# A residual block's second-norm sums and output scalings moved to ScalarE, with new plan latencies and weight slots

## The chip, the cores and the metric

The kernel runs on one core of a Trainium2 chip. The metric is device time in microseconds; lower is better. The core has five engines, each with its own in-order queue: TensorE (PE, matmuls; its weight loads are shown as PEld), VectorE (DVE), ScalarE (ACT), GpSimd (POOL) and SyncE (SP, which here issues most DMAs).

## The reference

A residual block of a diffusion network on two images of 512 channels, 64 x 64 pixels, in bf16:

```python
    B, C, H, W = x.shape                      # 2, 512, 64, 64
    G, eps = 4, 1e-5
    def gn(z, gamma, beta):                   # group norm, 4 groups of 128 channels
        ...
    def conv3(z, w):                          # 3x3 convolution, padding 1
        ...
    h = conv3(_silu(gn(x, g1, be1)), w1)
    emb = _silu(t_emb) @ w_emb
    h = h + emb.reshape(B, C, 1, 1)
    h = conv3(_silu(gn(h, g2, be2)), w2)
    return x + h
```

Each of the four groups is one block of 128 channels, so a group's mean and variance are sums over the free dimension of one tile followed by a sum over its 128 partitions.

## The kernel before, in words

**Arithmetic.** Both convolutions use a Winograd scheme along the rows: four output rows from six input rows, with the three taps along x kept as they are. A chunk is 32 rows of one image, so there are four chunks per layer (`chunks`, idx 0 to 3, two for each image). Layer 0 is the first convolution, layer 1 the second. For each chunk and each of the four blocks of output channels (`ot`) there is a set (`one_set`): six row positions, each a sum over four input blocks and three taps, 12 matmuls of 128 x 512. Positions come in pairs, (1,3), (2,4) and (0,5); a pair fills one of three accumulator tiles `acc` in PSUM, used in turn (`row_pair`, `next_acc`). In a plain set this makes 72 matmuls. In a column set (all of layer 1, and chunk 2 of layer 0, `COL0`), positions 0 and 5 are made by a second Winograd scheme along x, with half as wide matmuls (`col_pair`): 80 matmuls in all. In the last chunk of layer 1 the pair (1,3) is made that way too (`more_pair`): 88.

**The transformed input.** For each chunk and input block, `v_block` makes a block of `Vbuf`: group norm and Silu in one ACT instruction into `a_tmp` (`silu_rows`), then eight or more additions on DVE through `vt`, with some scalings on ACT or DVE (`make_v`). `Vbuf` holds two chunks.

**The transformed weights.** `u_blocks` takes two weight blocks at a time from `stage` (two buffers), transposes them on PE (nine transposes of 128 x 128 into `xa` and `xb`, line 348), copies them out with ACT (line 447), with scaled copies by 0.25 and 0.5 also read from PSUM by ACT (line 449), and forms the positions by additions on DVE into `Upair`, 22 slots of 128 columns per block. The middle tap and its half live in a temporary, `g1t`. `u_cols` and `u_more` form the slots for the column schemes. Layer 1's weights go where layer 0's were, as the last chunk of layer 0 is done with them.

**A set's output.** ACT evacuates pair (1,3) to `m1` and pair (2,4) to `w_`, scaled by 1/6. DVE forms sum and difference in `w_`; they are t1, t2 (sums) and s1, s2 (differences). Output rows 1 and 2 of each tile are s1 + 2 s2 and t1 + 4 t2; rows 0 and 3 are t1 + t2 and s1 + 8 s2 plus positions 0 and 5. In layer 0 these additions are `scalar_tensor_tensor` instructions on DVE that also give the sum of what they write (`acc_sum`, a column of `ssum`; line 292, each followed by an accumulator read), four in a plain set and six in a column set; those for positions 0 and 5 read `acc` in PSUM. In layer 1, where no sums are wanted, the factors 2, 4 and 8 are separate scalings on DVE (`ts`, line 284). After a layer-0 set the tile `y` goes out to `h_scr` by DMA, and ACT squares it in place for the sum of squares (`ssq`). In layer 1, POOL adds x by an accumulating DMA, and SP sends the result out.

**Statistics.** `first_stats` handles the first image's input with matmuls on PE (line 840). `second_stats` handles the second image's: for each input block and each half of 2048 pixels, one ACT Identity with a sum and one ACT Square with a sum, read from `V` into a scratch tile. `stats2` turns `ssum` and `ssq` into layer 1's norm. `norm` sums over partitions by a small fp32 matmul (line 364), followed by small DVE operations and a power on POOL (lines 377, 381) that end in the scale `sc` and the bias `nb`.

**The order.** Nothing is ordered by hand. Every instruction is first entered in a `_Plan` with its engine, an estimated cost, a latency `lat`, and what it reads and writes. `issue` runs a list scheduling eight times, keeps the order with the shortest planned span, and emits it: each engine's queue is thus fixed before the run. `lead` raises a node's priority. `wait` is added to the time at which a node may start after one of another engine. The parameters' DMAs on the ACT queue are planned with a latency of 2.0. The last set of all is `final_set`, written apart: it takes positions 2 and 4 one at a time, in that order, so that little is left behind the last matmul.

Of the kernel before, what the change touches and what calls it, by code (L numbers as in the profile page):

```python
# [18 lines left out]
class _Node:  # L19
    __slots__ = ("eng", "cost", "lat", "emit", "due", "idx", "pred", "succ", "left", "fin", "nbytes", "lead", "wait")  # L20


class _Plan:
# [39 lines left out]
    def add(self, eng, cost, emit, reads=(), writes=(), group=None, lat=0.09, due=None, nbytes=0, lead=0.0,  # L63
            wait=0.05):
        n = _Node()
        n.eng, n.cost, n.lat, n.emit, n.due, n.idx = eng, cost, lat, emit, due, len(self.nodes)
        n.nbytes, n.lead, n.wait = nbytes, lead, wait
# [24 lines left out]
        return n  # L92

    def _run(self, nodes, pred, succ, prio, look):
# [8 lines left out]
        while len(order) < len(nodes):  # L103
# [15 lines left out]
            if n.nbytes:  # L119
                dma = max(dma, s + 1.6) + n.nbytes / self.RATE  # L120
                fin = dma + 0.6
# [38 lines left out]
def kernel(  # L160
# [34 lines left out]
    NSL = 22  # L195
    COL0 = (2,)
# [55 lines left out]
    def small(shape, name):  # L252
        count["small"] += 1
        return sb(shape, f"{name}{count['small']}", F32)
# [41 lines left out]
    def act(out, in_, func=None, scale=1.0, bias=None, accum=None, **kw):  # L296
# [14 lines left out]
        plan.add("ACT", c, emit, reads, [out] + ([] if accum is None else [accum]), **kw)  # L311
# [44 lines left out]
    def norm(layer, b, c0, n, me, ps=None):  # L356
# [8 lines left out]
        plan.add("PE", 0.3, mm, [me[:], ones_neg[:]], tok if ps is None else [ps], lat=0.2, lead=100.0)  # L365
# [26 lines left out]
    Ut = [[[None] * CT for _ in range(CT)] for _ in range(2)]  # L392

# [6 lines left out]
    def u_cols(layer, ot, c0, n, tmp):  # L400
        U = u_pair(layer, ot, c0)
        two = lambda first: slots(U, c0, n, first, [[1, 2 * P]])
        ck = view(tmp, 0, [[2 * NKX * P, n], [1, 2 * P]])
        tt(ck, two(0), two(4), ALU.add)
        tt(two(6), ck, two(2), ALU.subtract)
        tt(two(20), ck, two(2), ALU.add)

    def u_more(layer, ot, c0, n):
        U = u_pair(layer, ot, c0)
        g = lambda kx: slots(U, c0, n, 8 + 4 * kx, [[2 * P, 2], [1, P]])  # L410
        ck = view(g1t, 0, [[2 * P, n], [P, 2], [1, P]])
        tt(ck, g(0), g(2), ALU.add)
        tt(slots(U, c0, n, 2, [[P, 2], [1, P]]), ck, g(1), ALU.subtract)
        tt(g(1), g(1), ck, ALU.add)

    def u_load(layer, ot, ct, **kw):
        k = count["blk"]
        count["blk"] += 1
        wn = stage[k % 2]
# [3 lines left out]
    def u_blocks(layer, ot, c0, loads, tmp=None, dve=False, act_scale=True):  # L423
# [3 lines left out]
        taps = [[P, NKX], [1, P]]  # L427
        for i, wn in enumerate(loads):
            ct = c0 + i
            Ut[layer][ot][ct] = U[:, ct % 2]  # L430
            one = lambda first, step: slots(U, ct, 1, first, [[step * P, NKX], [1, P]])
            raw = slots(U, ct, 1, 0, [[1, 6 * P]])
            mid = [view(tmp, (2 * i + h) * NKX * P, [[1, NKX * P]]) for h in range(2)]
            wv = wn[:].rearrange("p (c ky kx) -> p kx ky c", ky=3, kx=3)
            pa, pb = XBank("xa", [NKX, 2, P], BF16), XBank("xb", [NKX, P], BF16)
            transposes(pa, [((lambda t, kx=kx, j=j: t[:, kx, j, :]), wv[:, kx, 2 * j, :])
                            for kx in range(NKX) for j in range(2)], ["xa"], [wn[:]], 0.45)
            transposes(pb, [((lambda t, kx=kx: t[:, kx, :]), wv[:, kx, 1, :]) for kx in range(NKX)],
                       ["xb"], [wn[:]], 0.23)

            def copy(out, bank, tok, size_, sel=lambda t: t[:], scale=None):
# [3 lines left out]
                elif scale is None:  # L445
                    plan.add("ACT", 0.07 + size_ * 0.0008,
                             lambda: nc.scalar.copy(out=out, in_=sel(bank.get())), [tok], [out])  # L447
                else:
                    plan.add("ACT", 0.07 + size_ * 0.0008, lambda: nc.scalar.activation(
                        out=out, in_=sel(bank.get()), func=ACT.Copy, scale=scale), [tok], [out])  # L450
# [7 lines left out]
        g = lambda j: slots(U, c0, n, j, [[2 * P, NKX], [1, P]])  # L458
        up = lambda j: slots(U, c0, n, 8 + j, [[4 * P, NKX], [1, P]])
        m = lambda h: view(tmp, h * NKX * P, [[2 * NKX * P, n], [P, NKX], [1, P]])  # L460
        if dve or not act_scale:
            ts(up(3), g(0), 0.25)
            ts(m(1), m(0), 0.5)
        tt(up(1), g(0), g(1), ALU.add)
        tt(up(0), up(1), m(0), ALU.add)
        tt(up(1), up(1), m(0), ALU.subtract)
        tt(up(3), up(3), g(1), ALU.add)
        tt(up(2), up(3), m(1), ALU.add)
        tt(up(3), up(3), m(1), ALU.subtract)
# [3 lines left out]
    def u_tap(U, pos, kx):  # L473
        if pos in (0, NPOS - 1):
            return U[:, 2 * kx + (1 if pos else 0), :]
        return U[:, 8 + 4 * kx + pos - 1, :]

    def u_col(U, j, c):
        return U[:, (0, 20, 6, 4)[c] + j, :]

    def u_col_more(U, j, c):
        return U[:, (8 + 2 * j, 12 + 2 * j, 2 + j, 16 + 2 * j)[c], :]
# [82 lines left out]
    ssum = [small([CT, sum(6 if is_col(0, b, c) else 4 for c in range(NCH))], "ssum") for b in range(B)]  # L565
# [72 lines left out]
    def final_set(U, V):  # L638
# [15 lines left out]
        for k, pos in enumerate((2, 4)):  # L654
# [4 lines left out]
            if k == 0:  # L659
                for i in range(2):  # L660
                    tt(sd[:, i], sd[:, i], view(w_, i, [[2 * NFREE, 2], [2, NC]]), ALU.add)
# [12 lines left out]
        for h in range(2):  # L674
            o = view(y, h * n, [[(TH - 1) * W, 2], [TH * W, TR // 2], [1, W]])
            tt(o, o, view(w_, NFREE + h * NFREE // 2, [[2 * NFREE, 2], [1, NFREE // 2]]).rearrange(
# [4 lines left out]
    def one_set(layer, idx, ot, U, V):  # L681
# [7 lines left out]
        base = sum(6 if is_col(0, b, c) else 4 for c in range(ch))  # L689
# [4 lines left out]
        else:  # L694
            a = row_pair((1, 3), U, V, col, gid, 1)
            act(m1[:], a[:], scale=KAPPA)
# [23 lines left out]
        w03 = t4(w_[:, :, 0])  # L720
        if col and layer == 0:
            for k in range(2):
                tt(sd[:, k], sd[:, k], view(w_, k, [[2 * NFREE, 2], [2, NC]]), ALU.add)
        if not col:
            a = row_pair((0, 5), U, V, col, gid, 1)
            for i, f in enumerate((0, TH - 1)):
                stt(y4[:, f], t4(a[:, i:i + 1])[:, 0], 1.0, w03[:, i], ALU.mult, ALU.add, accum=acc_sum(2 + i))
        else:
            aa = col_pair((0, 3), U, V, gid)
            if layer == 0:  # L730
                for j in range(2):
                    for k, op in ((0, 1.0), (1, -1.0)):
# [3 lines left out]
                            accum=acc_sum(2 + 2 * j + k))  # L736
# [9 lines left out]
        y03 = y4[:, 0:TH:TH - 1]  # L746
        tt(y03, y03, w03, ALU.add)
# [3 lines left out]
    def emb_all():  # L751
# [5 lines left out]
        for e0 in range(0, ET, per):  # L757
            n = min(per, ET - e0)
            wt = stage[count["blk"] % 2]
            count["blk"] += 1  # L760
# [42 lines left out]
    for i, prm in enumerate((g1, be1, g2, be2)):  # L803
        o = gparm[CT * i:CT * (i + 1), :]
        plan.add("ACT", 0.1, lambda o=o, prm=prm: nc.scalar.dma_start(out=o, in_=prm.rearrange("(ct p) -> ct p", p=P)),
                 [], ["gp%d" % i], lat=2.0)
    plan.add("ACT", 0.1, lambda: nc.scalar.dma_start(out=tparm, in_=t_emb.rearrange("b (et p) -> (b et) p", p=P)),
             [], [tparm], lat=2.0)
# [15 lines left out]
    half = [view(g1t, 0, [[1, 2 * NKX * P]]), view(g1t, 2 * NKX * P, [[1, 2 * NKX * P]])]  # L824
# [49 lines left out]
    def second_stats(ct):  # L874
# [4 lines left out]
        for k in range(2):  # L879
            xin = X[:, k * HW // 2:(k + 1) * HW // 2]  # L880
            act(src[0][:, 0:HW // 2], xin, func=ACT.Identity, scale=1.0 / HW, accum=part[:, k:k + 1])
            act(src[0][:, 0:HW // 2], xin, func=ACT.Square, scale=float(HW) ** -0.5, accum=part[:, 2 + k:3 + k])
        tt(me[:], part[:, 0:4:2], part[:, 1:4:2], ALU.add)
        norm(0, 1, ct, 1, me)

    for layer in range(2):
        for idx, (b, ch) in enumerate(chunks):
# [3 lines left out]
            for ot in range(CT):  # L891
# [7 lines left out]
                if layer == 0 and idx == COL0[0] - 2:  # L899
# [61 lines left out]
```

## Time and profile before

| what | value |
|---|---|
| time, median of 3 runs | 529.96 us (528.39 to 530.06) |
| span of the profiled execution | 525.5 us |
| that execution's own total | not shown; the page gives its span alone |
| granted TensorE clock, mean | 0.998 |
| matmuls of line 576 | 2496 |
| DMA | 55.50 MB, 106 GB/s |

The span runs from the first to the last instruction; the time of a run is longer by what lies around it. A line of a group reads: line, engine, operation, what is written <- what is read, shapes, count, then busy time and the mean of one in ns, then the idle time of the engine just before such instructions and what ended it. A line of a waits view reads: who <- waited for whom: total us, times, longest. `L309`, `L279`, `L284` and `L292` are helpers' lines (`act`, `tt`, `ts`, `stt`), so groups are told apart by their tiles.

The transfers that the change touches, from the page's part on DMA issues (KB each, us to landing):

```profile
stage<-in_w_dram SPq DMA_DIRECT2D x32, 288.0 KB, 2.8
h_scr<-y SPq DMA_DIRECT2D x16, 512.0 KB, 2.7
V<-in_x_dram SPq DMA_DIRECT2D x6, 1024.0 KB, 7.5
```

### The profile page before, as it was taken

What the parts mean: (1) busy time and instruction counts of PE and PEld (TensorE: products, weight loads), DVE (VectorE), ACT (ScalarE), POOL (GpSimd) and SP (SyncE); (2) the same over time, 40 slices, a digit from 0 to 9 for tenths busy, and PEclk for the clock granted to TensorE, in tenths of its full rate; (3) what the DMA queues carried; (4) which work ended last, traced back from release to release, by engine and by line L of the source; (5) the groups of instructions that cost most, each with busy time, mean ns of one, the idle gap of its engine ahead of it and who ended that gap; (6) DMA issues with size and microseconds to landing.
All of it is one profiled execution on the core that took longest, in us unless ns stands there. A gap on an engine that the chain in (4) does not pass through costs nothing.

```text
span 525.5 us, 8039 instructions
## 1 busy us (share of the span) xinstructions
PE 499.6 (95%) x2986; PEld 276.3 (53%) x2986; DVE 464.4 (88%) x1048; ACT 333.4 (63%) x412; POOL 36.6 (7%) x83
## 2 busy tenths in 40 slices
PE   4888999999999899999989999999999999999994
PEld 4644554444444455555445465555555555567662
DVE  3898989977999997699999799987899999999766
ACT  4799998999854875667769695416555534333331
POOL 1210000011020200000000000021000000000010
PEclk9999999999999999999999999999999999999999
DMA  8302433541202322133333324533434534333434
GB/s 313 121 24 73 129 126 121 191 203 42 81 1 90 115 75 89 41 104 128 97 117 108 109 65 81 162 78 85 121 89 123 155 81 122 80 82 81 117 84 120
DMA packets 17313, 55.50 MB, mean 106 GB/s; under 512 B 1915, under 2 KB 3067, under 8 KB 16507
## 3 DMA queue, kind: packets, MB, share of 16 engines
q1 hardware_dynamic: 14912, 46.86, 26.1%
q0 software_dynamic: 2160, 7.87, 8.9%
q8 instruction: 23, 0.38, 0.3%
q10 hardware_dynamic: 203, 0.27, 0.1%
q14 instruction: 15, 0.12, 0.1%
HBM read 38.22 MB, written 16.78 MB: 105 GB/s over the span
## 4 chain that ended last, share of the span: by engine, by line
PE 57%; DVE 30%; ACT 6%; issue 3%; DMA 2%; POOL 1%; ACTq 0%; DVEq 0%
PE acc L576 54%; DVE V L279 8%; DVE vt L279 5%; DVE y L292 4%; ACT src L309 4%; DVE U L279 4%; DVE w L279 4%; PE xa L348 1%; DVE vt L284 1%; DVE y L279 1%; DMA V<-in_x_dram 1%; DMA mb<-in_be_dram 1%; ACT a_tmp L309 1%; PE acc L840 1%; POOL rstd L377 1%
## 5 line engine op out<-in xcount | busy, mean ns | idle before, releaser
L576 PE MATMUL acc<-V,U 128*128 128x512 bf16 (+1 forms) x2368 | 460.9, 352 | 6.5 <-DVE V L279 3.2
L576 PEld LDWEIGHTS <-U 128*128 128x128 bf16 x2496 | 240.9, 98 | 211.0 <-issue 8.6
L279 DVE TENSOR_TENSOR V<-vt 128x1056 bf16<-128x1056 bf16 (+2 forms) x124 | 83.6, 696 | 8.5 <-PE acc L576 5.1
L309 ACT ACTIVATE w<-acc 128x1024 bf16<-128x1024 f32 (+1 forms) x33 | 32.7, 990 | 39.9 <-PE acc L576 39.9
L279 DVE TENSOR_TENSOR w<-m,w 128x1024 bf16<-128x1024 bf16 (+1 forms) x66 | 44.2, 670 | 15.1 <-ACT w L309 14.3
L309 ACT ACTIVATE a_tmp<-src,nb,sc 128x2112 bf16<-128x2112 bf16 x20 | 42.7, 2147 | 22.5 <-DMA src<-h_scr 13.2
L309 ACT ACTIVATE m<-acc 128x1024 bf16<-128x1024 f32 x28 | 28.8, 1028 | 41.7 <-PE acc L576 40.2
L309 ACT ACTIVATE src<-vt 128x528 bf16<-128x528 bf16 x54 | 34.3, 638 | 25.6 <-DVE vt L279 25.6
L279 DVE TENSOR_TENSOR vt<-a_tmp 128x1056 bf16<-128x1056 bf16 x52 | 36.6, 704 | 4.8 <-ACT a_tmp L309 3.2
L279 DVE TENSOR_TENSOR U<-U,g1t 128x768 bf16<-128x768 bf16 (+2 forms) x76 | 36.4, 496 | 0.9
L447 ACT COPY U<-xa 128x768 bf16<-128x768 bf16 x31 | 24.9, 804 | 13.0 <-PE xa L348 8.4
L348 PEld LDWEIGHTS <-stage 128*128 128x128 bf16 x288 | 26.1, 143 | 11.5 <-DMA stage<-in_w_dram 1.3
L309 ACT ACTIVATE y<-y 128x2048 bf16<-128x2048 bf16 x16 | 30.6, 1912 | 1.9 <-DMA h_scr<-y 1.9
L309 ACT ACTIVATE src<-V 128x2048 bf16<-128x2048 bf16 x16 | 30.4, 1903 | 0.5 <-DMA V<-in_x_dram 0.3
L309 ACT ACTIVATE a_tmp<-V,nb,sc 128x2112 bf16<-128x2112 bf16 x12 | 25.9, 2154 | 4.6 <-DVE nb L292 4.6
L309 ACT ACTIVATE mb<-acc 128x1024 bf16<-128x1024 f32 x20 | 20.5, 1023 | 9.2 <-PE acc L576 6.4
L511 POOL MEMSET a_tmp<- 128x64 bf16 x32 | 5.2, 168 | 285.3 <-DVE vt L279 196.3
L279 DVE TENSOR_TENSOR vt<-vt,a_tmp 128x1056 bf16<-128x1056 bf16 x32 | 22.5, 704 | 0.4
L327 POOL DMA_DIRECT2D y<-in_x_dram x15 | 13.2, 879 | 131.1 <-DVE y L279 125.4
L279 DVE TENSOR_TENSOR w<-w 128x1024 bf16<-128x1024 bf16 x31 | 21.4, 689 | 0.7
L279 DVE TENSOR_TENSOR y<-sd,acc 128x512 bf16<-128x512 bf16 (+1 forms) x34 | 21.6, 685 | 0.2
L292 DVE SCALAR_TENSOR_TENSOR y<-w 128x512 bf16<-128x512 bf16 x32 | 21.0, 689 | 0.5
(107 smaller groups left out, 420.7 us busy)
## 6 DMA issues: line engine op xcount, KB each, us to landing
stage<-in_w_dram SPq DMA_DIRECT2D x32, 288.0 KB, 2.8
src<-h_scr SPq DMA_DIRECT2D x16, 528.0 KB, 3.8
h_scr<-y SPq DMA_DIRECT2D x16, 512.0 KB, 2.7
y<-in_x_dram POOLq DMA_DIRECT2D x15, 512.0 KB, 5.5
out_dram<-y SPq DMA_DIRECT2D x15, 512.0 KB, 2.6
V<-in_x_dram SPq DMA_DIRECT2D x6, 1024.0 KB, 7.5
src<-in_x_dram SPq DMA_DIRECT2D x4, 528.0 KB, 3.8
V<-in_x_dram SPq DMA_DIRECT2D x4, 512.0 KB, 6.5
```

What stands on the lines that cost most here:

```text
L279: lambda: nc.vector.tensor_tensor(out=out, in0=in0, in1=in1, op=op), [in0, in1], [out], **kw)
L284: nc.vector.tensor_scalar(out=out, in0=in_, scalar1=c, scalar2=None, op0=op)
L292: nc.vector.scalar_tensor_tensor(out=out, in0=in0, scalar=scalar, in1=in1, op0=op0, op1=op1, **extra)
L309: nc.scalar.activation(out=out, in_=in_, func=fn, scale=scale, **extra)
L327: q.dma_start(out=out, in_=in_, **extra)
L348: nc.tensor.transpose(sel(t), in_, ident[:in_.shape[0], :in_.shape[0]])
L377: pool(lambda: nc.gpsimd.tensor_scalar(out=rstd[:], in0=nvar[:], scalar1=-1.0, scalar2=EPS, op0=ALU.mult, op1=ALU.add), [nvar[:]], [rstd[:]])
L447: lambda: nc.scalar.copy(out=out, in_=sel(bank.get())), [tok], [out])
L511: pool(lambda r=r: nc.gpsimd.memset(rows[:, r, 1:W + 1], 0.0), [], [rows[:, r, 1:W + 1]], cost=0.2)
L576: nc.tensor.matmul(ap, lhsT=l, rhs=r, start=k == 0, stop=k == total[key] - 1)
L840: nc.tensor.matmul(gr, lhsT=blk, rhs=blk, start=(k == 0 and j == 0), stop=(k == 1 and j == 15))
```

## The change

Five edits come together.

- **Sums (layer 0).** ACT now makes the sums as it evacuates and scales: `m1` with the sum of both evacuated positions, 4 t2 and 2 s2 with theirs, and in plain sets the pair (0,5), which ACT copies into `sd` with its sum. The additions on DVE are plain `tensor_tensor` instructions. As the sums are of parts of the output, `stats2` weighs them by `swt` (4, 0.75, 4, and 1 for the rest), which POOL fills at the start. Column sets keep four `stt` with sums, and add `w03` to `y` afterwards instead of adding `w_` to `sd` before.
- **Scalings.** The factors 2, 4 and 8 are ACT instructions in both layers.
- **Second image's statistics.** Of each block's two plain sums the second (`DVE_SUMS`) is a `reduce_sum` on DVE; the division by the pixel count becomes a step of its own.
- **Plan.** The parameters' DMAs are planned with a latency of 5.5 (`PARAM_LAND`), and the statistics matmul of all norms but the first image's with a `wait` of 4.0 (`LATE`). The estimated costs of the transposes change from 0.45 and 0.23 to 0.4 and 0.2. A field `land` is new, and no call sets it.
- **Weight slots.** The order of the 22 slots is new: taps of one position lie together, and the middle tap has slots of its own. ACT's scaled copies are made from SBUF for two blocks at once, not from PSUM for each block. `g1t` is half as long, `stage` has three buffers, the many small tiles are cut from one (`arena`). In `final_set` position 4 goes ahead of position 2.

```diff
-    def add(self, eng, cost, emit, reads=(), writes=(), group=None, lat=0.09, due=None, nbytes=0, lead=0.0,
-            wait=0.05):
+            wait=0.05, land=0.0):
...
-                fin = dma + 0.6
+                fin = max(dma + 0.6, s + n.land)
...
+    SMALLS = 320
+    PARAM_LAND = 5.5
+    LATE = 4.0
+    DVE_SUMS = (1,)
...
-    stage = [sb([CQ], f"stage{i}") for i in range(2)]
+    stage = [sb([CQ], f"stage{i}") for i in range(3)]
-    g1t = sb([4 * NKX * P], "g1t")
+    g1t = sb([2 * NKX * P], "g1t")
+    arena = sb([SMALLS], "arena", F32)
...
-        plan.add("PE", 0.3, mm, [me[:], ones_neg[:]], tok if ps is None else [ps], lat=0.2, lead=100.0)
+        plan.add("PE", 0.3, mm, [me[:], ones_neg[:]], tok if ps is None else [ps], lat=0.2, lead=100.0,
+                 wait=0.05 if ps is not None else LATE)
...
@@ u_blocks
-            copy(raw.rearrange("p a (k o) -> p (a k) o", o=P).rearrange("p (kx j) o -> p kx j o", j=2),
-                 pa, "xa", 2 * NKX * P)
-            copy(mid[0].rearrange("p (k o) -> p k o", o=P), pb, "xb", NKX * P)
-            if act_scale and not dve:
-                copy(one(11, 4)[:, 0], pa, "xa", NKX * P, lambda t: t[:, :, 0, :], 0.25)
-                copy(mid[1].rearrange("p (k o) -> p k o", o=P), pb, "xb", NKX * P, scale=0.5)
+            copy(slots(U, ct, 1, 0, [[S_G2 * P, 2], [1, KP]])[:, 0], pa, "xa", 2 * KP, flat)
+            copy(one(S_MID, 1), pb, "xb", KP, lambda t: t[:].rearrange("p k o -> p (k o)"))
+        scaled(up(3), g(0), 0.25, act_scale and not dve)
+        scaled(half, mid, 0.5, act_scale and not dve)
...
@@ one_set
-            act(m1[:], a[:], scale=KAPPA)
+            if layer == 0:
+                act(m1[:], a[:], func=ACT.Identity, scale=KAPPA, accum=acc_sum(0))
+            else:
+                act(m1[:], a[:], scale=KAPPA)
...
         if layer == 0:
-            stt(y4[:, 1], t4(w_[:, 1, 1:2])[:, 0], 2.0, t4(w_[:, 1, 0:1])[:, 0], ALU.mult, ALU.add, accum=acc_sum(0))
-            stt(y4[:, 2], t4(w_[:, 0, 1:2])[:, 0], 4.0, t4(w_[:, 0, 0:1])[:, 0], ALU.mult, ALU.add, accum=acc_sum(1))
-            ts(s2, s2, 8.0)
+            act(m1[:, 1], t2, func=ACT.Identity, scale=4.0, accum=acc_sum(1))
+            act(m1[:, 0], s2, func=ACT.Identity, scale=2.0, accum=acc_sum(2))
         else:
-            ts(m1[:, 0], s2, 2.0)
-            ts(m1[:, 1], t2, 4.0)
-            ts(s2, s2, 8.0)
-            z12 = t4(m1[:])
-            tt(y4[:, 1], z12[:, 0], t4(w_[:, 1, 0:1])[:, 0], ALU.add)
-            tt(y4[:, 2], z12[:, 1], t4(w_[:, 0, 0:1])[:, 0], ALU.add)
+            act(m1[:, 0], s2, scale=2.0)
+            act(m1[:, 1], t2, scale=4.0)
+        act(s2, s2, scale=8.0)
+        z12 = t4(m1[:])
+        tt(y4[:, 1], z12[:, 0], t4(w_[:, 1, 0:1])[:, 0], ALU.add)
+        tt(y4[:, 2], z12[:, 1], t4(w_[:, 0, 0:1])[:, 0], ALU.add)
         tt(w_[:, :, 0], w_[:, :, 0], w_[:, :, 1], ALU.add)
         w03 = t4(w_[:, :, 0])
-        if col and layer == 0:
-            for k in range(2):
-                tt(sd[:, k], sd[:, k], view(w_, k, [[2 * NFREE, 2], [2, NC]]), ALU.add)
         if not col:
             a = row_pair((0, 5), U, V, col, gid, 1)
-            for i, f in enumerate((0, TH - 1)):
-                stt(y4[:, f], t4(a[:, i:i + 1])[:, 0], 1.0, w03[:, i], ALU.mult, ALU.add, accum=acc_sum(2 + i))
+            m05 = view(sd, 0, [[NFREE, 2], [1, NFREE]])
+            act(m05, a[:], func=ACT.Identity, accum=acc_sum(3))
+            tt(y4[:, 0:TH:TH - 1], t4(m05), w03, ALU.add)
...
+        y03 = y4[:, 0:TH:TH - 1]
+        if col:
+            tt(y03, y03, w03, ALU.add)
...
@@ stats2
+        tt(ssum[b], ssum[b], bass.AP(swt[b].tensor, swt[b].offset, [list(swt[b].ap[0]), [0, CT], list(swt[b].ap[1])]),
+           ALU.mult)
...
@@ final_set
-        for k, pos in enumerate((2, 4)):
+        for k, pos in ((1, 4), (0, 2)):
             a = row_pair((pos,), U, V, True, gid, 1)
...
-        act(m1[:, 0], w_[:, 1, 1], scale=2.0)
-        act(m1[:, 1], w_[:, 0, 1], scale=4.0)
-        ts(w_[:, 1, 1], w_[:, 1, 1], 8.0)
-        tt(y4[:, 1:3], y4[:, 1:3], t4(m1[:]), ALU.add)
+                continue
+            act(z[:, 0], w_[:, 1, 1], scale=2.0)
+            act(z[:, 1], w_[:, 0, 1], scale=4.0)
+            ts(w_[:, 1, 1], w_[:, 1, 1], 8.0)
+            tt(y4[:, 1:3], y4[:, 1:3], t4(z), ALU.add)
+            for i in range(2):
+                tt(sd[:, i], sd[:, i], view(w_, NFREE + i, [[2 * NFREE, 2], [2, NC]]), ALU.add)
...
@@ second_stats
-            act(src[0][:, 0:HW // 2], xin, func=ACT.Identity, scale=1.0 / HW, accum=part[:, k:k + 1])
+            if k in DVE_SUMS:
+                plan.add("DVE", 2.18, lambda xin=xin, o=part[:, k:k + 1]: nc.vector.reduce_sum(out=o, in_=xin, axis=AX.X),
+                         [xin], [part[:, k:k + 1]])
+            else:
+                act(src[0][:, 0:HW // 2], xin, func=ACT.Identity, accum=part[:, k:k + 1])
...
-        tt(me[:], part[:, 0:4:2], part[:, 1:4:2], ALU.add)
+        stt(me[:, 0:1], part[:, 0:1], 1.0, part[:, 1:2], ALU.mult, ALU.add)
+        ts(me[:, 0:1], me[:, 0:1], 1.0 / HW)
+        tt(me[:, 1:2], part[:, 2:3], part[:, 3:4], ALU.add)
```

More of the change, by code (lines that the diff above doesn't have):

```diff
@@ L19 @@
 class _Node:
-    __slots__ = ("eng", "cost", "lat", "emit", "due", "idx", "pred", "succ", "left", "fin", "nbytes", "lead", "wait")
+    __slots__ = ("eng", "cost", "lat", "emit", "due", "idx", "pred", "succ", "left", "fin", "nbytes", "lead", "wait", "land")
 class _Plan:
@@ L252, in small @@
     def small(shape, name):
-        count["small"] += 1
-        return sb(shape, f"{name}{count['small']}", F32)
+        n = 1
+        for d in shape:
+            n *= d
+        o = count["small"]
+        count["small"] += n
+        assert count["small"] <= SMALLS
+        return view(arena, o, [[shape[1], shape[0]], [1, shape[1]]] if len(shape) == 2 else [[1, n]])
     def size(a):
@@ L310, in act @@
         reads = [in_] + [a for a in (scale, bias) if a is not None and not isinstance(a, float)]
-        plan.add("ACT", c, emit, reads, [out] + ([] if accum is None else [accum]), **kw)
+        plan.add("ACT", kw.pop("cost", c), emit, reads, [out] + ([] if accum is None else [accum]), **kw)
     def scaled(out, in_, c, on_act):
@@ L426, in u_blocks @@
         U = u_pair(layer, ot, c0)
-        taps = [[P, NKX], [1, P]]
+        g = lambda j: slots(U, c0, n, j * S_G2, [[1, KP]])
+        mid = slots(U, c0, n, S_MID, [[1, KP]])
+        half = view(tmp, 0, [[KP, n], [1, KP]])
+        up = lambda j: slots(U, c0, n, S_UP + NKX * j, [[1, KP]])
         for i, wn in enumerate(loads):
@@ L430, in u_blocks, with copy @@
             Ut[layer][ot][ct] = U[:, ct % 2]
-            one = lambda first, step: slots(U, ct, 1, first, [[step * P, NKX], [1, P]])
-            raw = slots(U, ct, 1, 0, [[1, 6 * P]])
-            mid = [view(tmp, (2 * i + h) * NKX * P, [[1, NKX * P]]) for h in range(2)]
+            one = lambda first, m: slots(U, ct, 1, first, [[1, m * KP]])[:, 0]
             wv = wn[:].rearrange("p (c ky kx) -> p kx ky c", ky=3, kx=3)
-            pa, pb = XBank("xa", [NKX, 2, P], BF16), XBank("xb", [NKX, P], BF16)
-            transposes(pa, [((lambda t, kx=kx, j=j: t[:, kx, j, :]), wv[:, kx, 2 * j, :])
-                            for kx in range(NKX) for j in range(2)], ["xa"], [wn[:]], 0.45)
+            pa, pb = XBank("xa", [2, NKX, P], BF16), XBank("xb", [NKX, P], BF16)
+            transposes(pa, [((lambda t, kx=kx, j=j: t[:, j, kx, :]), wv[:, kx, 2 * j, :])
+                            for kx in range(NKX) for j in range(2)], ["xa"], [wn[:]], 0.4)
             transposes(pb, [((lambda t, kx=kx: t[:, kx, :]), wv[:, kx, 1, :]) for kx in range(NKX)],
-                       ["xb"], [wn[:]], 0.23)
-            def copy(out, bank, tok, size_, sel=lambda t: t[:], scale=None):
+                       ["xb"], [wn[:]], 0.2)
+            def copy(out, bank, tok, size_, sel):
                 if dve:
@@ L564 @@
     clock = {"t": T0}
-    ssum = [small([CT, sum(6 if is_col(0, b, c) else 4 for c in range(NCH))], "ssum") for b in range(B)]
+    cols_of = lambda b, c: 7 if is_col(0, b, c) else 4
+    ssum = [small([CT, sum(cols_of(b, c) for c in range(NCH))], "ssum") for b in range(B)]
+    swt = [small([sum(cols_of(b, c) for c in range(NCH))], "swt") for b in range(B)]
+    for b in range(B):
+        plan.add("POOL", 0.2, lambda b=b: nc.gpsimd.memset(swt[b], 1.0), [], [swt[b]])
+        for c in range(NCH):
+            o = sum(cols_of(b, k) for k in range(c))
+            for i, f in ((0, 4.0), (1, 0.75), (2, 4.0)):
+                plan.add("POOL", 0.2, lambda o=swt[b][:, o + i:o + i + 1], f=f: nc.gpsimd.memset(o, f), [],
+                         [swt[b][:, o + i:o + i + 1]])
     ssq = [small([CT, NCH], "ssq") for b in range(B)]
@@ L653, in final_set @@
         part = lambda i, k: t4(w_[:, i, k:k + 1])[:, 0]
-        for k, pos in enumerate((2, 4)):
+        z = view(stage[1], 0, [[NFREE, 2], [1, NFREE]])
+        for k, pos in ((1, 4), (0, 2)):
             a = row_pair((pos,), U, V, True, gid, 1)
@@ L688, in one_set @@
         y4 = yst[:].rearrange("p (t f w) -> p f t w", f=TH, w=W)
[L689 removed]
+        base = sum(cols_of(b, c) for c in range(ch))
         acc_sum = lambda i: ssum[b][:, ot, base + i:base + i + 1]
@@ L898 @@
                         u_more(1, ot, c0, 2)
-                if layer == 0 and idx == COL0[0] - 2:
+                if layer == 0 and idx == max(0, COL0[0] - 2):
                     for c0 in range(0, CT, 2):
```

71 lines of the change are left out of this document (31 added, 40 removed).

## The prediction

> **What bounds it now.** The page first: which engines are full over the whole span.
>
> ```profile
> span 525.5 us, 8039 instructions
> PE 499.6 (95%) x2986; PEld 276.3 (53%) x2986; DVE 464.4 (88%) x1048; ACT 333.4 (63%) x412; POOL 36.6 (7%) x83
> PE 57%; DVE 30%; ACT 6%; issue 3%; DMA 2%; POOL 1%; ACTq 0%; DVEq 0%
> ```
>
> The second line is busy time; the third is the chain that ended last, by engine. PE carries 57% of it and DVE 30%, but an average over two layers hides where. So the next view is busy time by stage. I cut at what the matmul starts of line 576 show: first set of chunk 0 from 20.3, chunk 1 of layer 0 from 101.8, chunk 2 from 166.1, chunk 3 from 224.5, layer 1 from 298.4, last matmul 518.5.
>
> ```profile
> 28.00:101.80 73.80, 69.97 (x428) 36.04 (x429) 67.35 (x154) 67.65 (x99) 2.38 (x9) 1.00 0.33 102
> 101.80:166.00 64.20, 63.88 (x301) 28.98 (x300) 56.24 (x142) 51.66 (x49) 6.18 (x12) 1.00 0.27 102
> 240.00:300.00 60.00, 56.61 (x338) 29.45 (x337) 54.46 (x120) 45.32 (x69) 0.31 (x2) 1.00 0.35 104
> 342.00:518.00 176.00, 176.00 (x1078) 104.56 (x1076) 159.50 (x325) 74.40 (x85) 15.00 (x25) 1.00 0.40 101
> ```
>
> Columns: stretch, its length, then busy PE, PEld, DVE, ACT, POOL, granted clock, DMA share, GB/s. From 342 to 518 PE is busy for all of 176.00 us: there matmuls alone set the time, and work taken off DVE buys nothing. In layer 0 DVE and ACT are both nearly full (67.35 and 67.65 of 73.8). What PE loses after its first set is read from its waits between 45 and 345 us:
>
> ```profile
> PE acc L576 <- DVE y L292: 3.1, 3, 1.4
> PE xb L364 <- DVE me L279: 2.1, 2, 1.9
> PE xa L348 <- DMA stage<-in_w_dram: 0.6, 1, 0.6
> PE acc L576 <- DVE V L279: 0.5, 1, 0.5
> PE xb L769 <- DVE emb_sb L774: 0.4, 1, 0.4
> PE xb L364 <- DVE emb_sb L776: 0.3, 1, 0.3
> ```
>
> Together 7.0 us. The largest is PE waiting for an accumulator that DVE's sum-carrying adds (line 292) have not yet read out; the second is a statistics matmul standing ahead of ready convolution work. The rest of the 525.5 is matmuls, a start in which little can run, and a tail of some 7 us behind the last matmul. So no edit off the matmuls can win much over ten microseconds.
>
> **The set's output (layer 0).** The rows:
>
> ```profile
> L292 DVE SCALAR_TENSOR_TENSOR y<-w 128x512 bf16<-128x512 bf16 x32 | 21.0, 689 | 0.5
> L292 DVE SCALAR_TENSOR_TENSOR y<-acc,w 128x512 bf16<-128x512 f32 x24 | 16.1, 688 | 1.1 <-PE acc L576 0.3
> L279 DVE TENSOR_TENSOR y<-m,w 128x512 bf16<-128x512 bf16 x30 | 11.3, 418 | 0.0
> L284 DVE TENSOR_SCALAR w<-w 128x512 bf16<-128x512 bf16 x32 | 9.2, 287 | 0.0
> L309 ACT ACTIVATE m<-w 128x512 bf16<-128x512 bf16 x2 | 1.1, 621 | 1.0 <-DVE w L279 1.0
> L309 ACT ACTIVATION_READ_ACCUMULATOR src<-V 128x1 f32 x16 | 3.0, 187 | 0.0
> L847 DVE TENSOR_REDUCE part<-V 128x1 f32<-128x1024 bf16 x2 | 2.4, 1213 | 0.0
> ```
>
> A plain set (12 of 16) loses on DVE four adds with a sum, 4 x (0.69 + 0.08 for the accumulator read) = 3.08, and the scaling by 8, 0.29: 3.37 in all. It gains two 512 adds, 0.84, and one 1024 add over packed bf16, 0.69 by the w<-w row: 1.53. DVE saves 1.84 us. ACT gains three scalings, 3 x 0.62, the copy of (0,5) out of the accumulators, 1.02 by the rows of m and w, and four accumulator reads, 4 x 0.19: 3.64 us. Back to back ACT instructions overlap (the 528 row lasts 0.64 and its successor starts 0.53 later), so what ACT really loses lies between 2.95 (eight instructions, 0.09 less each) and 3.64. A column set (4 of 16) keeps its four strided adds: DVE loses 1.54 + 0.29 + 1.37 (two strided adds into sd), gains 1.53, so saves 1.67; ACT gains 3 x 0.62 + 3 x 0.19 = 2.4.
>
> What this frees is the accumulators. (0,5) is now released by an ACT copy that needs no DVE result before it, so the 3.1 us of waiting for line 292 goes if ACT comes in time. Ends: 0 (ACT late instead) to -3.1; I take **-2.5**, since ACT has to be late by a whole row pair (24 matmuls, 5.2 us) before PE feels it.
>
> **Second image's statistics.** Each block's second half goes from an Identity on ACT, 1.90 + 0.19, to a DVE reduction of 2048: 2 x 1.21 = 2.4 as upper bound, 1.9 if half of the shorter one were fixed cost. Four of them: ACT -8.4, DVE +7.6 to +9.7. DVE was idle for 4.34 us in one piece at 116 to 120, waiting for an ACT copy. Two more small DVE operations per block cost 0.4 us each time, ahead of normalisations whose V blocks ended at 164.5, 1.5 us before PE wanted them.
>
> **What ACT then holds.** From 28 to 166 it was busy 67.65 + 51.66 = 119.3 of 138.0 us, idle 18.7. Eight sets add 24 to 29, the statistics take 8.4 off, and the scaled weight copies (four of 0.52 a pair become two of 768 elements, 0.83 between the 528 and 1056 rows) take 0 to 0.4 off for each of six pairs. That leaves 16 to 19 us more: ACT becomes full to within 0 to 3 us. DVE loses 14.7 and gains 8.6 there, so it is a little freer. Not all of ACT's idle time can be filled, since it waited for data:
>
> ```profile
> ACT a_tmp L309 <- DVE vt L279: 5.6, 1, 5.6
> ACT src L309 <- DVE vt L279: 2.5, 2, 2.4
> ```
>
> If half of the 18.7 can't, ACT ends 16 + 9.4 - 18.7 = 6.7 us late. Against that, the squares (2.1 us each) may trail by up to three output buffers, 6.3 us, and the V blocks of chunk 1 were ready some 8 us early. Ends 0 to +6.7; I take **+1.5**. Around 240 to 300 ACT goes from 45.3 to about 58 of 60 and DVE from 54.5 to 47; the weight blocks that fill ACT there are needed only as layer 1 reaches them, 298 to 343, where ACT had 15 us idle. I put **+0.5** (0 to +2).
>
> The Trainium skill, "ScalarE: Activation LUTs", section "Rules for kernel authors", says that multiplies belong on VectorE, not ScalarE, which is up to about three times slower in bf16. The rows agree, 0.62 against 0.29. By that rule alone the 48 layer-0 and 45 layer-1 scalings cost 93 x 0.33 = 31 us of engine time, an estimate. "Perfetto Trace Analysis", section "Optimizing Scalar/DVE Operations", allows the move where DVE is saturated and so speaks for it only where ACT isn't.
>
> **Layer 1.** Fifteen sets move 0.29 x 3 = 0.87 us from DVE to 3 x 0.62 on ACT: DVE -13, ACT +28. Cover: PE, without a gap from 342; ACT goes there from 74 to about 97 of 176. **0.** Without that cover the chain evacuate, subtract, scale, add is 3 x 0.33 = 1 us longer per set.
>
> **The plan's latencies.** Statistics matmuls are now planned 4 us behind their operands, so that PE isn't parked at them: 2.1 us go, ends 0 to -2.1 (177.0, waiting 1.88, is nearly all of it); I take **-1.9**. At the start PE's queue stood at the parameters' transpose:
>
> ```profile
> 6.60 0.17 PE L813 MATMUL xb<-ident,mb 16*128 16x16 bf16 x1 [6.60 <-DMA mb<-in_be_dram]
> 11.42 0.30 DVE L292 SCALAR_TENSOR_TENSOR acc<-acc,ident 128x128 f32<-128x128 f32 x1 [1.21 <-PE acc L840]
> ```
>
> The first weights, issued at 0.74, landed within 3.1 us, the first half of x by 5.77 (ACT starts on it), so with the transpose planned later PE does nine transposes and half the 32 statistics matmuls before 8. DVE, 1.21 us idle before 11.42, then waits for its own reduction instead: the first Silu (14.92, ACT idle 1.70 before it) comes about 1.1 earlier. After it DVE is nearly full, so the shift is kept: **-1.0** (-1.9 to 0; the parameters' scale is needed only at 14.5).
>
> **Weights.** A third staging buffer lets SP issue one load further ahead; the 0.6 us wait for a stage goes: **-0.6** (0 to -0.6). Transposes, copies and adds keep number and size. Fourteen memsets on POOL, 0.1 to 0.2 each, lie in its idle first 10 us (1.83 busy); without that cover, 2 us before the first rstd at 13.5.
>
> **Tail.** With position 4 first, 0.68 and 0.29 of DVE work leave the stretch behind the last row matmul and one 0.42 add enters: -0.55. Ahead of it DVE has 0.89 + 0.29 + 1.36 + 0.69 = 3.2 us beside 2.6 of matmuls, up to +0.6. **-0.3**.
>
> Sum: -2.5 + 1.5 + 0.5 - 1.9 - 1.0 - 0.6 - 0.3 = -4.3. The span goes from 525.5 to 521.2. No total is shown for the profiled execution; the median of the runs, 529.96, is 4.5 above its span, and I carry that over: **525.7**.
>
> **Rivals.**
> A. ACT becomes the bound of chunks 0 and 1 of layer 0: +6.7, and the 3.1 us of accumulator waits stay, now waiting for ACT. The others bring -1.9 - 1.0 - 0.6 - 0.3 = -3.8. Then 529.96 + 2.9 = 532.9, slower. It decides once ACT's unfillable idle time passes some 6 us. For: 98 to 100% full. Against: squares and V blocks can slide. 0.20.
> B. The waits move: a new order of all engines puts others, of equal size, where the 7.0 us were, and only the start is gained: 529. For: every queue is fixed beforehand, from planned times. Against: the causes of 5.6 of the 7.0 are named and removed. 0.14.
> C. A freer DVE also fills the first set, which takes 26.3 us (20.3 to 46.6) for 72 matmuls, 15.7 us of work, with transposes 17.5: if 3 of those 8.8 go, and ACT costs nothing: 525.7 - 3 - 2 = 520.7. For: PE waits there for V. Against: the change takes no DVE work out of that set before 46. 0.18.
> D. The longer chain through the single m1 buffer stalls layer 1: from the evacuation of (2,4), 1.0 + 1.4 + 1.24 + 0.84 = 4.5 us until m1 is free, against 6.9 us of matmuls until the next is due. With queues of over 2.4 us on ACT it slips, and at 0.5 us in 15 sets costs 7.5: 533.2. ACT at half load speaks against. 0.04.
>
> The forecast's own case holds 0.44, from 523 to 528.3. Range: C's best end (all terms at their good ends, -8.3, and 3 in the first set) is 518.7; A is 532.9 and D 533.2: 518.5 to 533. A measurement tells 0.3%, 1.6 us, from no change: faster takes the forecast's case almost whole, and C: 0.62; same is B and a rest: 0.15; slower is A and D, nearly: 0.23.
>
> **What will show it.** Right: no PE wait for line 292's y; no wait over 0.5 us at the statistics matmuls; PE's first transpose near 4 us; ACT over 95% and DVE under 85% between 28 and 166; chunk 2 starting before 166.1; layer 1 as long as before (298.4 to 518.5, 220). Wrong: PE waiting for ACT copies in 60 to 170, or gaps after 342.

## The result, and the profile after

The changed kernel takes 528.34 us (median of 20 runs, 526.18 to 530.10), the kernel before 530.25 (20 runs): a ratio of 0.9957, 95% interval 0.9943 to 0.9972. It is faster by 1.5 to 3 us, some half of what was forecast.

The page of the changed kernel (span, busy time by engine):

```profile
span 525.5 us, 8020 instructions
PE 500.0 (95%) x2986; PEld 276.9 (53%) x2986; DVE 448.1 (85%) x929; ACT 386.2 (73%) x541; POOL 36.7 (7%) x97
```

The span equals that of before, though the medians differ. Every listed run has its time and its span, and they differ by about 2 us (1.7 to 2.2; this one 527.42 and 525.5). So the profile of before, with the same span, came from an execution of about 527.5, just below its kernel's 20 listed runs (527.83 to 532.29). Two single profiles can't show a difference of 2 us in their totals; they are read by stages here. Busy time by stage, columns as before:

```profile
28.00:101.80 73.80, 69.51 (x424) 35.33 (x423) 65.12 (x135) 69.85 (x106) 2.06 (x9) 1.00 0.33 102
101.80:166.00 64.20, 64.20 (x306) 29.69 (x305) 57.35 (x128) 59.46 (x78) 6.83 (x12) 1.00 0.24 91
240.00:300.00 60.00, 58.76 (x354) 31.03 (x353) 55.81 (x109) 56.59 (x92) 0.46 (x3) 1.00 0.39 118
342.00:518.00 176.00, 174.21 (x1065) 103.36 (x1063) 149.00 (x278) 95.74 (x125) 15.46 (x24) 1.00 0.41 101
```

ACT went from 119.3 to 129.3 us in the first two stretches, DVE only from 123.6 to 122.5, and PE gained in the third, 56.6 to 58.8. PE's waits between 45 and 345 us:

```profile
PE acc L592 <- DVE y L302: 2.6, 2, 2.4
PE xb L358 <- DMA stage<-in_w_dram: 1.2, 1, 1.2
PE xb L358 <- DVE arena L378: 0.9, 1, 0.9
PE xb L787 <- DVE emb_sb L794: 0.3, 1, 0.3
PE acc L592 <- DVE V L289: 0.3, 1, 0.3
PE xb L358 <- ACT U L463: 0.3, 1, 0.3
```

The sum is 5.6 us, against 7.0. The wait for the statistics matmul's operand is gone, though one of 0.9 is new at a transpose that needs the bank `xb`, until line 378 has copied such a matmul's result out of it. And the wait for the accumulators that DVE reads in line 302 (formerly 292) is nearly as long as before, 2.6 against 3.1. It is another wait now. Before, its three parts stood in plain sets (0.84 us at 84.05, 1.42 at 272.33, 0.79 at 297.75); now it is in chunk 2, the column sets:

```profile
198.99 0.63 ACT L319 ACTIVATE m<-w 128x512 bf16<-128x512 bf16 x1 [2.49 <-DVE w L289]
...
200.23 0.61 ACT L319 ACTIVATE w<-w 128x512 bf16<-128x512 bf16 x1
...
200.75 2.14 ACT L319 ACTIVATE a_tmp<-src,arena 128x2112 bf16<-128x2112 bf16 x1
...
202.91 0.71 DVE L289 TENSOR_TENSOR vt<-a_tmp 128x1056 bf16<-128x1056 bf16 x1 [1.34 <-ACT a_tmp L319]
...
204.97 0.44 DVE L302 SCALAR_TENSOR_TENSOR y<-acc,sd 128x256 bf16<-128x256 f32 x1
...
205.47 4.99 PE L592 MATMUL acc<-V,U 128*128 128x512 bf16 x26 [2.36 <-DVE y L302]
```

These lines of the timeline are to be read from below: PE stood 2.36 us for an accumulator that DVE's adds with a sum had to read; those stood in DVE's queue behind a V block's first subtraction, which had waited 1.34 us for ACT's Silu (200.75). Ahead of the Silu ACT had the three scalings (198.99 to 200.84), and the first of them had waited 2.49 us for DVE's sum and difference in `w_`.

### The profile page after: what moved, and what is told of

It is laid out like the page before. It is cut to its first block, busy times and chain, and to the rows that moved or that the text cites. A ratio compares the mean times of both kernels' runs of the same rounds, so it can differ in the third digit from the quotient of the medians.

```text
span 525.5 us, 8020 instructions
## 1 busy us (share of the span) xinstructions
PE 500.0 (95%) x2986; PEld 276.9 (53%) x2986; DVE 448.1 (85%) x929; ACT 386.2 (73%) x541; POOL 36.7 (7%) x97
## 4 chain that ended last, share of the span: by engine, by line
PE 39%; DVE 22%; ACT 13%; issue 3%; DMA 2%; POOL 2%; DVEq 0%; ACTq 0%; SPq 0%
PE acc L592 38%; DVE V L289 6%; DVE vt L289 5%; DVE w L289 4%; ACT src L319 4%; ACT a_tmp L319 3%; DVE y L289 3%; ACT m L319 3%; ACT w L319 2%; POOL arena L392 1%; DMA stage<-in_w_dram 1%; DMA src<-h_scr 1%; DVE sd L289 1%; PE xa L358 1%; DVE vt L294 1%
## 5 line engine op out<-in xcount | busy, mean ns | idle before, releaser
L289 DVE TENSOR_TENSOR V<-vt 128x1056 bf16<-128x1056 bf16 (+2 forms) x124 | 84.8, 696 | 6.7 <-PE acc L592 4.6
L319 ACT ACTIVATE m<-w 128x512 bf16<-128x512 bf16 x62 | 37.5, 625 | 26.2 <-DVE w L289 22.2
L319 ACT ACTIVATE a_tmp<-src,arena 128x2112 bf16<-128x2112 bf16 x20 | 42.8, 2141 | 4.3 <-DMA src<-h_scr 2.6
L289 DVE TENSOR_TENSOR U<-U 128x768 bf16<-128x768 bf16 (+1 forms) x72 | 35.6, 509 | 3.7 <-ACT U L319 2.0
L289 DVE TENSOR_TENSOR y<-m,w 128x512 bf16<-128x512 bf16 x62 | 25.9, 423 | 11.5 <-ACT m L319 9.5
L319 ACT ACTIVATE a_tmp<-V,arena 128x2112 bf16<-128x2112 bf16 x12 | 25.8, 2149 | 2.0 <-DVE arena L302 2.0
L289 DVE TENSOR_TENSOR U<-U,g1t 128x768 bf16<-128x768 bf16 (+2 forms) x42 | 20.7, 492 | 3.4 <-ACT g1t L319 2.6
L289 DVE TENSOR_TENSOR w<-w 128x1024 bf16<-128x1024 bf16 x31 | 21.4, 689 | 2.0
L319 ACT ACTIVATE src<-V 128x2048 bf16<-128x2048 bf16 x12 | 22.8, 1901 | 0.1
```

Source lines behind the costliest of these rows:

```text
L289: lambda: nc.vector.tensor_tensor(out=out, in0=in0, in1=in1, op=op), [in0, in1], [out], **kw)
L319: nc.scalar.activation(out=out, in_=in_, func=fn, scale=scale, **extra)
```

## The experiments

What a stage lost is worked out from the matmul and transpose rows: for each, the time between its end and the end of the one before it on PE, beyond what it takes back to back (0.22 us for 512 columns, half for 256), added up where over 0.03. "Start" is set 0's first matmul, "tail" the span behind the last one. These columns come from one profiled execution of each kernel. Times are medians; the ratio is to the kernel before on the same chip, which had 530.32, 530.15 and 530.63 in the three groups (E1 to E4, E5 to E8, E9 to E12).

| kernel | time | ratio (95%) | start | set 0 | sets 1-3 | chunk 1 | chunk 2 | chunk 3 | layer 1 | tail |
|---|---|---|---|---|---|---|---|---|---|---|
| before | 530.25 | 1 | 20.3 | 6.1 | 2.1 | 1.1 | 2.2 | 4.3 | 0.5 | 7.0 |
| E5, lead 16 | 531.13 | 1.0023 (1.0001-1.0045) | 22.9 | 6.1 | 1.9 | 1.2 | 2.1 | 3.2 | 4.0 | 7.0 |
| E1, both latencies | 527.74 | 0.9945 (0.9925-0.9966) | 22.7 | 7.8 | 2.6 | 1.3 | 0.6 | 4.2 | 0.1 | 7.0 |
| E7, 4.0 alone | 525.71 | 0.9913 (0.9886-0.9940) | 22.3 | 6.1 | 1.3 | 1.3 | 0.6 | 4.2 | 0.1 | 7.0 |
| E12, 4.0, lead 16 | 525.12 | 0.9885 (0.9853-0.9917) | 20.1 | 6.1 | 1.7 | 1.3 | 0.7 | 1.4 | 1.0 | 7.0 |
| changed | 528.34 | 0.9957 (0.9943-0.9972) | 21.6 | 5.9 | 0.9 | 0.3 | 4.5 | 1.5 | 1.3 | 8.2 |
| E2, without 4.0 | 530.20 | 1.0007 (0.9982-1.0032) | 21.5 | 8.4 | 1.4 | 1.6 | 4.1 | 1.1 | 1.0 | 8.2 |
| E3, parameters 2.0 | 526.80 | 0.9935 (0.9911-0.9959) | 23.1 | 5.4 | 1.7 | 0.3 | 3.7 | 0.0 | 0.5 | 8.2 |
| E4, last set | 527.08 | 0.9933 (0.9910-0.9956) | 22.9 | 5.9 | 1.0 | 0.3 | 4.5 | 1.1 | 1.2 | 7.1 |
| E6, lead 16 | 522.27 | 0.9859 (0.9831-0.9886) | 20.9 | 5.5 | 1.0 | 0.4 | 3.1 | 0.2 | 0.1 | 8.2 |
| E8, old outputs | 524.51 | 0.9894 (0.9867-0.9921) | 21.7 | 8.1 | 1.0 | 0.3 | 2.1 | 0.5 | 0.7 | 8.2 |
| E9, lead 14 | 527.33 | 0.9938 (0.9914-0.9961) | 20.8 | 8.5 | 1.4 | 0.3 | 3.7 | 0.0 | 0.1 | 8.2 |
| E10, lead 16, without 4.0 | 526.04 | 0.9913 (0.9886-0.9941) | 21.4 | 6.5 | 0.6 | 1.7 | 2.9 | 0.4 | 1.4 | 8.2 |
| E11, lead 16, last set | 521.20 | 0.9816 (0.9785-0.9848) | 21.5 | 5.1 | 1.0 | 0.4 | 3.1 | 0.0 | 0.1 | 7.1 |

**E1 and E7: the latencies alone, in the kernel before.** The edit of E7; E1 also has the parameters' 5.5.

```diff
-    ... tok if ps is None else [ps], lat=0.2, lead=100.0)
+    ... tok if ps is None else [ps], lat=0.2, lead=100.0, wait=0.05 if ps is not None else 4.0)
```

> The kernel before, with the changed plan latencies alone (parameters 5.5 instead of 2.0, statistics matmuls 4.0 behind their operands); all work as before. Theory L (the gain comes from the latencies, the moved work gives nothing): 1.5 to 3 us faster than before, PE waits at the statistics matmuls (2.1 us between 45 and 345) gone, first Silu about 1 us earlier. Theory W (the gain comes from the sums and scalings moved to ScalarE): within 1 us of before. Theory R (any edit that makes the planner deal a new order moves the time by 2 us either way, and the gain is one draw of that): anywhere from -3 to +3, without relation to those waits.

> The kernel before with the statistics matmuls planned 4.0 us behind their operands, nothing else (the parameters' latency stays 2.0). Theory L, and the parameters' latency of no use: 2.5 to 4 us faster than before, no PE wait over 0.5 us at the statistics matmuls after 45 us. Theory R: no relation to the 3 us that both latencies together gave; anywhere from -3 to +3.

E1 is 2.9 us faster than before by the ratio, E7 4.6, with none of the work moved. That is on the side of theory L, and against W: the latencies alone give at least as much as the whole change. PE's waits of E7 between 45 and 345:

```profile
PE acc L576 <- DVE y L292: 3.3, 4, 1.3
PE acc L576 <- DVE V L279: 1.8, 3, 0.7
PE xa L348 <- DMA stage<-in_w_dram: 0.5, 1, 0.5
PE xb L769 <- DVE emb_sb L776: 0.2, 1, 0.2
```

The 2.1 us at the statistics matmuls (L364) are gone, and nothing of that size took their place: the longer wait for V is mostly set 0's, which ran 2.0 us later here and so reaches into the window (0.44 and 0.68 at 44.77 and 46.45; 42.78 and 44.45 before). But the gain is more than those 2.1 us.

**E2 and E10: the changed kernel without the latency of 4.0**, in its own order and with the lead of 16 (`LATE = 0.05`).

> The changed kernel with the statistics matmuls planned right behind their operands again (0.05 instead of 4.0). Theory L: 1 to 2 us slower than the changed kernel, about 1 us faster than before, with some 2 us of PE waits at the statistics matmuls back. Theory W: within 0.7 us of the changed kernel. Theory R: 2 us either way.

> The changed kernel with the lead of 16 and the statistics matmuls planned right behind their operands (0.05). Theory L (the latency is worth 2 us or more in any order): 3 to 6 us slower than with the lead of 16 alone, 525 to 528.5 us or more. Theory R: may as well be equal or faster.

Both lose: E2 all of the gain, more than theory L's 1 to 2 us, and E10 0.5% of E6's 1.4%. So in four pairs that differ by this latency (before and E7, E5 and E12, E2 and the changed kernel, E10 and E6) the kernel with it is faster each time, by 0.9, 1.4, 0.5 and 0.5%. Each pair also differs in its order, which moves the time by up to 1.0% on its own (E5, E6 and E9 below), so four of four is strong support and not a proof.

**E3: the changed kernel with the parameters planned at 2.0 again** (`PARAM_LAND = 2.0`).

> The changed kernel with the parameters' DMAs planned with a latency of 2.0 again. Theory L: about 1 us slower than the changed kernel, PE's first transpose at 6.6 us again and first Silu near 14.9 instead of 13.75. Theory W: within 0.7 us. Theory R: 2 us either way.

It is not slower but 1.2 us faster by the ratios, with intervals that overlap; in the kernel before (E7 against E1) the old value is faster too. This part of the change gained nothing.

**E5, E6 and E9: the order alone** (`TURN` 16 or 14 for 15, the priority lead of the transposes and of the embedding's small matmuls; no instruction changes).

> The kernel before with the transposes' priority lead of 16 us instead of 15: no instruction changes, only the order that the planner deals (about a tenth of PE's places, two thirds of DVE's and ScalarE's). Theory L (the planned latency of 4.0 itself removes PE's stalls): within 0.8 us of before. Theory R (a new order is a draw, and the latency was one such draw): moves by 1.5 to 3 us, either way.

> The changed kernel with that lead of 16 instead of 15, again the order alone. Theory L: within 0.8 us of the changed kernel, 1 to 2.5 us faster than before. Theory R: 1.5 to 3 us off the changed kernel, either way.

> The changed kernel with the transposes' lead of 14 instead of 15 (16 made it 6 us faster): the order alone. Theory R (the order is a draw): anywhere from 522 to 531 us, and not in line with 15 and 16. Theory G (a larger lead is better as such): slower than the changed kernel, 529 to 533.

E5 is 1.2 us slower than before, between its two expectations; E9 is 1.0 us faster than the changed kernel, E6 5.2 us (all by the ratios). One step of one priority is worth more than the whole change, and 14, 15, 16 are in no line: theory R holds beside L. E6's waits between 45 and 345 sum to 2.8 us:

```profile
PE xb L358 <- ACT U L463: 1.2, 1, 1.2
PE acc L592 <- DVE y L302: 1.1, 2, 0.9
PE xb L787 <- DVE emb_sb L794: 0.5, 2, 0.3
```

Against the changed kernel's list the DMA wait and the one for L378 are not there, line 302's fell from 2.6 to 1.1, and the one for ACT's copy rose from 0.3 to 1.2. E5 shows the other side, in its own list for the same stretch: without the 4.0, a new order parked PE twice as long at the statistics matmuls (before: 2.1), 1.82 of it in layer 1.

```profile
PE xb L364 <- DVE me L279: 4.2, 3, 1.8
```

**E8: layer 0's outputs as before, all else changed.** `one_set` has its four `stt` with sums, `ts` by 8 and the adds into `sd` again where `layer == 0`, and the weights `swt` are all 1.

> The changed kernel with layer 0's outputs as before: sums made by VectorE's adds, its scalings and the copy of (0,5) off ScalarE; layer 1's scalings stay on ScalarE, weight slots, latencies and second statistics as changed. If the sums on ScalarE brought my 2.5 us of accumulator waits net of 2.0 for a full ScalarE: 0.5 us slower than the changed kernel. If they cost more than they gave, as the kernel before with latencies alone suggests: 0.5 to 1.5 us faster than the changed kernel, with 3 to 5 us of PE waits for VectorE's sum-carrying adds.

It is 3.3 us faster than the changed kernel by the ratios, more than expected, with 1.8 us of waits for those adds, fewer than expected. Chunk 2 loses 2.1 us instead of 4.5, and chunk 3 still only 0.5. In the plain sets, where the new outputs were to free the accumulators, E8 has no such wait either. With orders moving the time by 5 us, the 3.3 can't be credited to the outputs, but it is no sign of a gain from them.

**E12: the kernel before with 4.0 and lead 16**, to tell order from work.

> The kernel before with the latency of 4.0 and the lead of 16: no work changed. If the 522 us of the changed kernel with a lead of 16 is owed to the order alone, this comes near it: 521 to 524. If the changed kernel's weight slots and outputs are worth their 3 us in chunk 3 and 2 in the first sets in any order: 525 to 528, with chunk 3 at 74 us again, against 70 to 71 for all kernels with the new slots.

525.12 us, 0.1 inside the second expectation's times and 1.1 outside the first's. Chunk 3 lost 1.4 us in this order (it took 70.9 us), not the 74 that the second theory wanted: the old slots can do nearly as well there. Three pairs compare all of the moved work with the old, with the 4.0 in both. With lead 16 (E6 and E12) the changed work is ahead by 0.0026 of the ratio, 1.4 us, but E6 has the parameters' 5.5 and E12 has 2.0. At lead 15 it is behind, by 1.2 us with 2.0 in both (E3 and E7) and by 0.6 us with 5.5 in both (the changed kernel and E1). The intervals overlap in all three.

**E4 and E11: the last set's evacuation.**

```diff
-            act(w_[:, 1, k], a[:, 0], scale=KAPPA)
-            tt(w_[:, 0, k], m1[:, k], w_[:, 1, k], ALU.add)
-            tt(w_[:, 1, k], m1[:, k], w_[:, 1, k], ALU.subtract)
+            ev = view(stage[2], k * NFREE, [[1, NFREE]]); act(ev, a[:, 0], scale=KAPPA)
+            tt(w_[:, 0, k], m1[:, k], ev, ALU.add)
+            tt(w_[:, 1, k], m1[:, k], ev, ALU.subtract)
```

> The changed kernel; in the last set alone ScalarE evacuates positions 4 and 2 into the spare staging buffer instead of into w. PE's, POOL's and SP's orders are the same, DVE's and ScalarE's change in the last set only. Theory F (the last evacuation, 516.18, waits for the adds into sd only because a strided view that spans its target counts as overlapping it): that evacuation starts about 0.9 us after the one in the changed kernel's queue would have been free, 0.6 to 1.2 us faster than the changed kernel. Theory D (DVE has that much to do behind the last matmul in any case): within 0.4 us.

> The changed kernel with the lead of 16 and the last set's evacuations into the staging buffer; PE's order is that of the lead of 16. The stretch behind the last matmul goes from 8.2 to 7.1 us: 521.2 us, 1.1 faster than the lead of 16 alone. If the tail's gain were an accident of that run: 522.3.

The last evacuation in the timeline of the changed kernel, then of E4:

```profile
516.18 0.60 ACT L319 ACTIVATE w<-acc 128x512 bf16<-128x512 f32 x1 [1.15 <-DVE sd L289]
```

```profile
516.30 0.60 ACT L319 ACTIVATE stage<-acc 128x512 bf16<-128x512 f32 x1 [0.38 <-PE acc L592]
```

In the first it waits for DVE's add into sd, in the second for PE alone. The last matmul ended at 517.25 and 518.07, so in E4 the evacuation comes 0.7 us earlier against it, and the tail is 7.1 us instead of 8.2, in E11 too. That bears theory F out: the add reads `w_` through a strided view whose elements lie beside the evacuation's target, but whose span covers it. By the ratios E4 is 1.3 us faster than the changed kernel and E11 2.3 us faster than E6 (1.1 by the medians), with intervals that overlap. E11 is the fastest version: 521.20 us.

## Why the prediction was right in sign and too large

Direction and range held; the forecast of -4.3 us met -1.5 to -3. By E2 and E7 the sign came from the smaller half of the forecast, the plan's latency of 4.0. The term that was to bring most, the accumulators, was not shown to bring anything. That the result lay as near as it did is partly luck: one step of the lead, with the same work, gives 522.27 us. Step by step:

- **What bounds it.** Right: PE's own work fixed the result to some ten microseconds; layer 1 took 218.7 to 220.8 us in all kernels but E5. Wrong was taking the profiled execution for a typical one: 4.5 us around the span were really 2.0, and 2.5 were that run's luck.
- **The accumulator waits, -2.5.** Right for plain sets in what was seen, not shown in its cause. The 3.1 us before stood in plain sets, and none of the eight kernels with the new outputs waits there for such an add. But E8, with the old outputs and all else changed, doesn't either. The step that failed is the bad end, "0 (ACT late instead)": it allows for PE waiting for ACT, but not for the four column sets, which keep DVE's adds from PSUM and now have them behind a longer chain through ACT. All eight kernels with the new outputs lost 2.9 to 4.5 us in chunk 2; with the old outputs and the 4.0 it was 0.6 or 0.7 (E1, E7, E12) and 2.1 (E8). From before to the changed kernel the loss in chunk 2 grew by 2.3 us, more than any other column.
- **ACT full, +2.0.** Too dear as a direct cost. ACT gained 10.0 us between 28 and 166, not 16 to 19 (the prediction's own terms add up to 13 to 21), and was busy 129 of 138 us. PE waited for ACT itself for 0.3 us between 45 and 345, but the 2.36 us in chunk 2 came from ACT by way of DVE. Single durations were right (scaling 0.62, copy of (0,5) 1.01 in the rows). Rival A didn't happen.
- **The plan: statistics, -1.9.** Right in mechanism: PE's waits for these matmuls' operands after 45 us are gone wherever the 4.0 stands. In the changed kernel 0.9 came back as the wait for line 378. Its size in the changed kernel, 2.6 us by E2, and 4.6 in the kernel before, hold a share that is a new order and not those waits; how much of them is open.
- **The plan: parameters, -1.0.** In the profiled execution the first Silu came 1.17 us earlier as worked out (13.75), and DVE kept the shift: its first two V additions ended at 18.84 and 19.58, against 20.22 and 21.35. Yet nothing was gained. The step that failed is to price DVE's shift ("so the shift is kept") as PE's. PE's queue, dealt anew, held other work ahead of the first convolution matmul, which began 1.3 us later than before:

```profile
19.91 0.38 PE L374 MATMUL acc<-arena,ones_neg 128*128 128x2 f32 x2 [0.71 <-DVE acc L302]
...
20.15 1.05 PE L860 MATMUL acc<-V 128*128 128x128 bf16 x16
...
21.04 0.34 PE L358 MATMUL xb<-ident,stage 128*128 128x128 bf16 x3
21.22 0.52 PE L358 MATMUL xa<-ident,stage 128*128 128x128 bf16 x6
...
21.59 0.60 PE L592 MATMUL acc<-V,U 128*128 128x512 bf16 x2
```

By the start of chunk 1 the changed kernel was 0.6 us ahead of before (101.2 against 101.8). That is less than the start varies by itself: E4, in the same PE order, got there at 102.5, and E3, with the old 2.0, at 102.9. In the kernel before with the 4.0, E1 (5.5) got there at 105.7 and E7 (2.0) at 103.2.

- **Weights, -0.6.** Not as named: the wait for a stage was 1.2 us in the changed kernel, against 0.6, though it is gone in E3 and E6. Chunk 3 gained more, but 2.2 of the 4.3 us that it lost before are waits for accumulators, which the prediction counts under its first term. The nine kernels with the new slots and third buffer lost 0 to 1.5 us in chunk 3, the five without 1.4 to 4.3. E12's 1.4 shows that the order has a part in it, and E8's 0.5 that the outputs aren't needed for it; how much is the slots' is open.
- **Layer 1, 0.** Nearly: one wait of 1.04 us for a V block (404.52) in the changed kernel, none in E6. DVE was relieved by 10.5 us there, and nothing came of it, as forecast.
- **Tail, -0.3.** Wrong: +1.2. The reordering put the sd add's view across the last evacuation's target, which E4 shows to cost 1.1. Without it the tail is 7.1 against 7.0, so the 0.3 didn't come either.
- **Its signs.** Those for the plan came: no wait over 0.5 us for the statistics matmuls' operands from 45 us on, the first transpose at 3.62, chunk 2 from 164.9, layer 1 219.9 us long. Those for the outputs didn't: PE waits at line 302, ACT is busy 94% and DVE 89% between 28 and 166, and there is a gap after 342.

The rule that multiplies belong on VectorE (the Trainium skill, "ScalarE: Activation LUTs", "Rules for kernel authors") holds for one instruction, 0.62 against 0.29 here. The scalings' 31 us of engine time, as the prediction estimated it, show in PE's waits only in chunk 2.

Rival B came nearest among the others: waits did move, to chunk 2 and the tail. C and D didn't happen: set 0 lost 5.9 us against 6.1, and layer 1 took no longer. That the sums on ScalarE are worth anything in themselves was not shown: the changed work lies between 1.2 us behind the old and 1.4 ahead.

## What to carry to other kernels

Where a planner deals a fixed order, any edit is also a new draw of that order: run a few neutral draws (a priority moved by one) of both versions before a difference of 1% is credited to the work. Plan what an in-order engine will wait for, late rather than early: in four pairs of four here, small statistics matmuls parked at the head of PE's queue cost more than a plan that expects them 4 us later. And when an output path is moved off an engine, look at the variant that keeps the old path (here the column sets): its work now waits for both engines.

## What the runs showed of the chip beside that

The same order starts at different times: set 0's first matmul came at 21.6 and 22.9 us in the changed kernel and E4, and at 20.9 and 21.5 in E6 and E11, whose PE orders are the same in pairs. In the first pair it is the landing of x: ScalarE's sum over a later part of it, held by that transfer in both, began at 8.42 and at 9.80. And the time goes with the mean granted clock, which lay between 0.986 and 0.998 in all runs: over the 114 runs of the changed kernel and the twelve variants, each about its own kernel's mean, 0.001 less went with 0.43 us more, which accounts for less than half of the scatter. Both effects are as large as those sought here, and an average over runs is needed for either.
